# Attention and a PReLU MLP on one Trainium2 core: the first batch taken by halves of its queries, with a new order of the opening

## The chip, the cores and the metric

The kernel runs on one core of one Trainium2 chip. TensorE (PE) multiplies matrices and writes its results to PSUM; VectorE (DVE) and ScalarE (ACT) do element-wise work and read PSUM; GpSimd (POOL) does element-wise work in SBUF and issues part of the DMAs; SyncE (SP) issues the others. Every engine works off its own queue strictly in the order in which the kernel recorded its instructions. The metric is the device time of one execution in microseconds (us), as the median of several runs.

## What is computed

```python
q_n, k_n = rmsnorm(q, g_q), rmsnorm(k, g_k)          # (8, 12, 448, 64), over the last axis
attn = softmax(q_n @ k_n.T / 8);  o = attn @ v        # per batch and head
x = o.transpose(0, 2, 1, 3).reshape(3584, 768)
h = x @ w_in                                          # (768, 2048)
g = max(h, 0) + alpha * min(h, 0)
out = g @ w_out                                       # (2048, 768), float32
```

## The kernel before, in words

Each of the 8 batches has 12 heads, taken in three *groups* of four; group y is number y % 3 of batch y // 3, so groups 0, 1 and 2 are batch 0. The 448 queries or keys of a head are seven sets of 64. Everything is issued by a list of steps, PLAN (lines 24 to 190), that fixes the order on all engines at once. A step has a name, and its arguments say which group, set or column block it works on:

- `load_qk(y)` (line 286): q and k of a group by DMA from SP's queue, 448 KB each. A load waits until its buffer's last reader is done. `load_v`, `load_w_in(c)` (335), `load_w_out`: DMAs from POOL's queue that also turn the values into 16 bits. `load_w_in(c)` brings rows 0 to 511 of a quarter of w_in's columns in four DMAs and, for an even c, rows 512 to 767 of two quarters in four more.
- `square` (361; on POOL, in one case on ACT), `reduce` (378; DVE), `root` (408; ACT), `scale` (419; DVE or POOL), `turn` (543), `turn_one` (509): rms norm of a group's q and k and their transposes on PE, with copies out of PSUM on DVE. For group 0 the pieces are finer: `part_square`, `part_reduce`, `part_root`, `part_scale`, `part_turn`, `part_copy` (446 to 501).
- `opening` (1010): the first loads, the small DMAs of alpha, g_q and g_k into `rows`, idle matmuls (`spin`, 996: 2 wide float32 ones and 17 narrow 16-bit ones), and a transpose `ct` of `rows`; `gains` (1028) makes the product g_q * g_k, by which k is multiplied as it is copied to kT.
- `score(y,j)` (580): for key set j, the products with all 448 queries, for the group's four heads: four matmuls of 64x64 weights and 448 columns. `soft(y,j)` (599): exp on ACT, 128x896 values. Seven of each per group.
- `den` (645), `attend` (675): sums over the keys of exp, and of exp times v, with 64x32 weights; 56 matmuls each. Groups 0 and 1 are summed together ("0+1", with two `attend`), group 2 alone. `log` and `invert` (ACT) make 1/den as exp(-ln), `times` (693; DVE) multiplies and writes xT, the MLP's input, as 16 bits.
- `up(b,ft)` (746): one block of 128 of the 2048 hidden values for 448 tokens: six matmuls of 128x128 weights and 448 columns. `begin(ft)` (734) does the first four of the six ahead, from groups 0+1 alone. `slope` (757; ACT, three blocks on DVE) writes alpha*h, `larger` (770; DVE) the maximum of h and that. `down(tile,oh)` is the second product.

PSUM has eight banks in three pools: `pss`, two buffers of two banks, for scores; `psa`, one of two banks; `psf` (tag "mm"), two of one bank. The last argument of `score`, `den`, `attend` and `up` chooses the pool. A step that asks for a buffer waits until its last reader is done.

Of the kernel before, what the change touches and what calls it, by code (L numbers as in the profile page):

```python
# [20 lines left out]
GROUPS = ("den", "den_pre", "log", "log_pre", "invert", "attend", "times")  # L21
# [3 lines left out]
opening() part_square(q,0:1,0:7,act) part_square(q,1:2,0:7,act) part_reduce(q,0:1,0:7) spin(2,0)  # L25
part_reduce(q,1:2,0:7) part_root(q,0:7) part_square(k,0:2,0:3,act) part_scale(q,0:7,7,pool)
part_reduce(k,0:2,0:3) part_square(k,0:2,3:7,act) square(1,q) load_w_in(1) spin(1)
part_reduce(k,0:2,3:7) part_root(k,3:7) reduce(1,q) square(1,k) part_root(k,0:3) gains()
part_turn(q,r0-7) load_qk(3) spin(1,0) part_scale(k,0:3,3,vec) part_turn(k,r0-3)
part_scale(k,3:7,4,vec) part_copy(q,0:7,vec) part_turn(k,r3-7) load_v(0) reduce(1,k) follow(0,k)  # L30
square(2,q) part_copy(k,0:3,vec) part_copy(k,3:7,vec) root(1) square(2,k) score(0,0,0) soft(0,0)
reduce(2,q,0) score(0,4,1) load_w_in(0) score(0,3,0) spin(1) reduce(2,q,1) soft(0,3) score(0,1,0)
scale(1,k) scale(1,q) soft(0,4) score(0,2,0) soft(0,2) reduce(2,k) score(0,6,1) turn_one(1,q)
soft(0,1) turn_one(1,k) score(1,0,1) score(1,3,0) spin(1) score(1,2,0) soft(0,6) root(2) soft(1,0)
load_qk(4) soft(1,3) scale(2,k) scale(2,q) follow(2,q) square(3,q) square(3,k) load_w_in(2)
soft(1,2) score(0,5,1) score(1,1,0) soft(0,5) soft(1,1) score(1,5,0) turn(2) soft(1,5) score(1,6,1)
soft(1,6) reduce(3,q,None) score(1,4,0) score(2,0,0) soft(1,4) den(0+1,0) follow(1,k) soft(2,0)
log(0+1) load_qk(5) score(2,1,0) spin(1) reduce(3,k,0+1) attend(0+1,1,0) score(2,6,0) score(2,4,1)
attend(0+1,0,1) soft(2,1) root(3) score(2,3,1) invert(0+1) scale(3,q) scale(3,k) score(2,2,0)
load_w_in(3) soft(2,4) soft(2,6) times(0+1,1,0) times(0+1,1,1) square(4,q) times(0+1,0,0) turn(3)  # L40
score(2,5,0) square(4,k) load_qk(6) reduce(4,q,None) soft(2,3) soft(2,2) soft(2,5) den(2,0) log(2)
reduce(4,k,None) invert(2) attend(2,0,1) score(3,0,1) square(5,q) square(5,k) times(2,0,0)
score(3,1,0) begin(0) reduce(5,q) square(6,q) soft(3,0) begin(1) up(0,0,0) load_w_out(0) reduce(5,k)
up(0,1,0) begin(2) begin(3) root(4) up(0,2,0) up(0,3,1) up(0,4,0) scale(4,q) slope(0,0) soft(3,1)
larger(0,0) score(3,2,0) score(3,6,0) slope(0,1) load_qk(7) follow(2,k) larger(0,1) slope(0,4)
slope(0,2) slope(0,3) larger(0,4) up(0,5,0) larger(0,2) larger(0,3) root(5) soft(3,6) slope(0,5)
soft(3,2) larger(0,5) up(0,6,0) scale(4,k) turn(4) scale(5,q) up(0,8,0) score(4,0,0) slope(0,6)
score(4,1,1) square(6,k) larger(0,6) slope(0,8) score(3,5,0) up(0,9,0) load_w_out(1) scale(5,k)
soft(4,0) square(7,q) larger(0,8) up(0,11,0) load_qk(8) score(4,2,0) score(3,3,0) soft(3,5)
load_v(1) square(7,k) up(0,7,1) soft(4,1) slope(0,9) up(0,10,0) reduce(6,q) square(8,q) reduce(6,k)  # L50
load_w_out(2) soft(4,2) up(0,12,0) slope(0,11) larger(0,9) soft(3,3) score(3,4,0) slope(0,10)
score(4,3,0) larger(0,11) larger(0,10) slope(0,7) larger(0,7) up(0,13,0) soft(3,4) slope(0,12)
larger(0,12) turn(5) up(0,14,0) square(8,k) soft(4,3) score(4,6,0) slope(0,13) score(4,4,1) root(6)
slope(0,14) larger(0,13) up(0,15,0) scale(6,q) reduce(8,q) soft(4,4) score(5,4,0) larger(0,14)
scale(6,k) score(5,0,1) reduce(7,q) slope(0,15) larger(0,15) down(1,0,0) score(5,2,1) score(4,5,0)
soft(4,6) soft(5,0) soft(5,4) soft(5,2) score(5,1,0) soft(4,5) down(0,0,0) turn(6) load_w_out(3)
den(3+4,1) reduce(7,k) attend(3+4,0,0) score(5,5,0) score(5,6,0) soft(5,1) mix_weights(0,1) log(3+4)
invert(3+4) soft(5,5) soft(5,6) mix_weights(0,3) attend(3+4,1,0) score(6,0,1) score(5,3,0) soft(6,0)
score(6,4,0) down_end(0,0) down(2,0,0) soft(5,3) root(7) scale(7,q) load_qk(9) soft(6,4) scale(7,k)
den(5,0) attend(5,0,1) down_end(1,0) mix_weights(0,2) times(3+4,0,0) times(3+4,1,0) times(3+4,1,1)  # L60
load_qk(10) log(5) down(0,1,0) reduce(8,k) invert(5) down_end(2,0) times(5,0,1) times(5,0,0)
times(5,0,3) times(5,0,2) score(6,5,1) mix_weights(0,0) score(6,1,0) down_end(0,1) score(6,6,0)
soft(6,5) turn(7) up(1,1,1) square(9,q) down(1,1,0) root(8) reduce(9,q) soft(6,6) score(6,3,1)
score(7,0,0) slope(1,1) score(6,2,0) up(1,2,0) up(1,0,0) soft(6,1) soft(7,0) soft(6,3) square(9,k)
up(1,3,1) up(1,4,0) slope(1,2) slope(1,0) larger(1,1) down_end(1,1) reduce(9,k) root(9) larger(1,2)
load_qk(11) larger(1,0) slope(1,3) scale(8,q) soft(6,2) up(1,7,0) slope(1,4) larger(1,3) larger(1,4)
scale(8,k) score(7,4,0) slope(1,7) larger(1,7) up(1,5,1) scale(9,q) turn(8) score(7,5,0) soft(7,4)
score(7,1,0) up(1,6,0) square(10,q) slope(1,5) larger(1,5) up(1,10,0) soft(7,5) soft(7,1) up(1,8,1)
scale(9,k) up(1,9,0) reduce(10,q) score(7,2,0) slope(1,6) slope(1,10) larger(1,6) mix_weights(1,1)
score(7,6,0) slope(1,8) slope(1,9) soft(7,6) up(1,12,1) up(1,11,0) soft(7,2) square(10,k) up(1,13,0)  # L70
larger(1,8) larger(1,10) slope(1,12) score(7,3,0) larger(1,9) up(1,14,1) slope(1,11) slope(1,13)
mix_weights(1,3) reduce(10,k) up(1,15,0) load_v(2) soft(7,3) larger(1,12) load_qk(12) score(8,3,0)
score(8,0,0) den(6+7,0) slope(1,14) fold(10) root(10) slope(1,15) soft(8,0) down(2,1,0) larger(1,11)
larger(1,13) square(11,q) log(6+7) score(8,1,0) score(8,4,0) soft(8,3) flip(9,k) scale(10,q)
larger(1,14) larger(1,15) score(8,5,1) mix_weights(3,1) down_end(2,1) reduce(11,q) square(11,k)
# [16 lines left out]
soft(10,5) slope(2,13) larger(2,6) larger(2,8) larger(2,10) reduce(13,k) up(2,11,0) larger(2,5)
larger(2,12) load_qk(15) score(11,0,0) fold(13) den(9+10,1) slope(2,11) mix_weights(3,3) qa1(6,0)
up(2,15,0) qa2(6,1) root(13) mix_weights(3,0) flip(12,q) slope(2,9) larger(2,14) larger(2,13)
down(5,0,0) log(9+10) slope(2,15) larger(2,11) larger(2,9) invert(9+10) soft(11,0) square(14,k)
# [98 lines left out]
def kernel(  # L194
# [903 lines left out]
```

## Time and profile before

| | |
|---|---|
| median of 3 runs | 411.36 us (410.83 to 411.58) |
| the profiled execution | 410.69 us, of which the span is 408.6 us |
| busy: PE, DVE, ACT, POOL | 97%, 66%, 66%, 73% of the span |
| HBM read, written | 58.40 MB, 11.01 MB |

Busy time is the time in which an engine has an instruction at work; matmuls overlap each other, so a group's busy time can be less than count times mean. PEld is the weight load of PE, which runs beside its matmuls. In the timeline a line gives start, busy time, engine, source line, operation, tiles and shape, the number of merged instructions, and in brackets the engine's idle time before them with what ended it. Idle time of an engine that does not bound the kernel costs nothing.

### The profile page before, as it was taken

Reading aid. Unit: us, or ns where it says so; the run is one execution under the profiler, and the core shown is the slowest. Engines: PE = TensorE matmul, PEld = TensorE weight load, DVE = VectorE, ACT = ScalarE, POOL = GpSimd, SP = SyncE. Lnnn points to the kernel's source line nnn. Section 1 sums busy time; section 2 is a strip of 40 time slices with the busy share of each in tenths; the row PEclk is TensorE's granted clock in tenths of the full one; section 3 lists DMA queues with packets and bytes.
Section 4 is the critical chain, followed back from the end, with each engine's and each line's share of the span. In section 5 each row is a group of like instructions: output and inputs, shape, how many; then the busy total and the mean of one; then the engine's idle time right before and its main releaser. Section 6 shows DMA issues by size and latency. Waiting matters only on the chain.

```text
span 408.6 us, 11992 instructions
## 1 busy us (share of the span) xinstructions
PE 395.3 (97%) x5083; PEld 210.3 (51%) x5083; DVE 268.3 (66%) x480; ACT 270.4 (66%) x405; POOL 299.9 (73%) x200
## 2 busy tenths in 40 slices
PE   7688999999999999999999999999999999999996
PEld 3344445555455445554455455555555455655664
DVE  3957874676766685779678678886668545654422
ACT  5597686757885876767886987686876874245110
POOL 7977998497796998997796995589496809600780
PEclk9999999999999999999999999999999999999999
DMA  7999699796776794579952595794516000230143
GB/s 260 242 280 227 110 265 165 173 239 177 125 180 154 173 203 108 119 172 185 232 130 83 136 240 145 147 217 102 140 38 131 21 2 22 59 79 0 39 98 98
DMA packets 37222, 58.39 MB, mean 143 GB/s; under 512 B 4769, under 2 KB 28977, under 8 KB 37169
## 3 DMA queue, kind: packets, MB, share of 16 engines
q1 hardware_dynamic: 23232, 45.43, 43.2%
q0 software_dynamic: 13536, 11.81, 19.1%
q8 instruction: 39, 0.64, 0.7%
q10 hardware_dynamic: 400, 0.39, 0.3%
q14 instruction: 15, 0.11, 0.1%
HBM read 58.40 MB, written 11.01 MB: 170 GB/s over the span
## 4 chain that ended last, share of the span: by engine, by line
PE 88%; DVE 4%; DMA 3%; POOL 3%; issue 1%; POOLq 0%; DVEq 0%
PE hT L726 25%; PE hTa L726 9%; PE sc L588 8%; PE op L792 7%; PE qx L854 5%; PE av L613 5%; PE qz L854 4%; PE qc L854 4%; PE oq L854 4%; PE qxa L854 3%; PE avb L613 2%; PE dn L613 2%; PE oqm L854 2%; DMA w_in_sb<-in_moe_w_in_dram 2%; POOL nat L376 2%; DMA arena<-in_g_k_dram 2%
## 5 line engine op out<-in xcount | busy, mean ns | idle before, releaser
L602 ACT ACTIVATE expT<-sc 128x896 f16<-128x896 f32 x168 | 146.3, 916 | 40.9 <-PE sc L588 39.2
L726 PE MATMUL hT<-xT,w_in_sb 128*128 128x448 f16 x558 | 115.9, 353 | 1.6 <-DVE xT L709 1.4
L726 PEld LDWEIGHTS <-w_in_sb 128*128 128x128 f16 x768 | 73.0, 98 | 74.5 <-issue 9.9
L423 POOL TENSOR_TENSOR qs<-nat,rr 128x896 f16<-128x896 f32 x30 | 65.7, 2221 | 26.5 <-ACT rr L417 23.4
L766 ACT ACTIVATE gT<-hT,cols 128x448 f16<-128x448 f32 x92 | 58.4, 636 | 40.0 <-PE hT L726 38.9
L772 DVE TENSOR_TENSOR gT<-hT,gT 128x448 f16<-128x448 f32 x93 | 57.3, 619 | 38.2 <-ACT gT L766 37.5
L365 POOL TENSOR_TENSOR nat<-nat 128x896 f32<-128x896 f32 x30 | 50.7, 1697 | 8.1 <-DMA nat<-in_q_dram 7.7
L588 PE MATMUL sc<-qT,kT 64*32 64x448 f16 (+1 forms) x1092 | 49.4, 355 | 4.3 <-ACT expT L602 1.7
L854 PEld LDWEIGHTS <-gT 128*128 128x128 f16 x352 | 33.4, 98 | 25.5 <-issue 4.1
L726 PE MATMUL hTa<-xT,w_in_sb 128*128 128x448 f16 x198 | 42.9, 353 | 0.0
L842 POOL TENSOR_TENSOR gs<-gT 128x1024 f16<-128x1024 f16 x4 | 8.5, 2127 | 36.7 <-DVE gT L772 36.7
L709 DVE TENSOR_TENSOR xT<-av,rden 64x448 f16<-64x448 f32 (+1 forms) x37 | 27.2, 736 | 10.7 <-ACT rden L671 4.6
L386 DVE TENSOR_REDUCE sp<-nat 128x28 f32<-128x896 f32 x30 | 32.1, 1070 | 2.1 <-POOL nat L365 2.0
L588 PEld LDWEIGHTS <-kT 64*32 64x32 f16 (+1 forms) x1092 | 16.7, 93 | 32.4 <-issue 23.0
L792 PE MATMUL op<-w_out_sb,gT 128*128 128x384 f16 x176 | 30.3, 326 | 0.2 <-DVE xT L709 0.2
L766 ACT ACTIVATE gT<-hTa,cols 128x448 f16<-128x448 f32 x33 | 21.0, 636 | 10.5 <-PE hTa L726 10.0
L772 DVE TENSOR_TENSOR gT<-hTa,gT 128x448 f16<-128x448 f32 x33 | 20.4, 618 | 10.6 <-ACT gT L766 10.2
L613 PEld LDWEIGHTS <-vt 64*32 64x32 f16 x1344 | 19.7, 92 | 12.2 <-issue 1.9
L792 PEld LDWEIGHTS <-gT 128*128 128x128 f16 x192 | 18.3, 98 | 14.5 <-issue 3.0
L613 PE MATMUL av<-expT,vt 64*32 64x448 f16 x896 | 24.3, 350 | 0.0
L850 POOL TENSOR_TENSOR gT<-gT 128x1024 f16<-128x1024 f16 x11 | 23.5, 2133 | 0.0
L854 PEld LDWEIGHTS <-arena 128*128 128x128 f16 x136 | 12.6, 98 | 10.5 <-issue 2.3
(151 smaller groups left out, 572.5 us busy)
## 6 DMA issues: line engine op xcount, KB each, us to landing
nat<-in_q_dram SPq DMA_DIRECT2D x60, 216.0 KB, 4.1
nat<-in_k_dram SPq DMA_DIRECT2D x60, 216.0 KB, 5.0
out_dram<-osb SPq DMA_DIRECT2D x107, 96.0 KB, 3.1
vt<-in_v_dram POOLq DMA_DIRECT2D x8, 672.0 KB, 7.8
w_in_sb<-in_moe_w_in_dram POOLq DMA_DIRECT2D x24, 128.0 KB, 7.3
w_out_sb<-in_moe_w_out_dram POOLq DMA_DIRECT2D x4, 768.0 KB, 8.6
nat<-in_k_dram SPq DMA_DIRECT2D x6, 448.0 KB, 7.8
nat<-in_q_dram SPq DMA_DIRECT2D x5, 448.0 KB, 6.7
```

Source lines behind the costliest of these rows:

```text
L365: nc.gpsimd.tensor_mul(out=sqs[y, nm], in0=t[:, :, :HD], in1=t[:, :, :HD])
L386: nc.vector.tensor_reduce(out=parts[y][:, ts("qk".index(nm), 4 * J), :1], in_=sqs[y, nm], axis=AXIS_X, op=ALU.add,)
L423: nc.gpsimd.tensor_mul(out=t.rearrange("p j d n -> p n j d"), in0=nat[y, nm][:, :, :HD].rearrange("p (n j) d -> p n j d", j=J), in1=r.unsq ...
L588: nc.tensor.matmul(out=sc[ds(64 * g + m * c, m), par, :S].rearrange("p (j c) -> p j c", j=J), lhsT=kT[ds(64 * par, 64), j, g, ts(c, m)], r ...
L602: nc.scalar.activation(out=expT[y][:, j], in_=scs[y, j][:, :, :S], func=AF.Exp, scale=QK_SCALE, bias=EXP_BIAS,)
L613: nc.tensor.matmul(out=accs[g][ds(32 * n, 32), :S], lhsT=weights(g, y, par, c, j), rhs=expT[y][ds(64 * g, 64), j, par, :], start=(j == 0), ...
L709: nc.vector.tensor_mul(out=o, in0=p, in1=q)
L726: nc.tensor.matmul(out=hT[:, :S], lhsT=w_in_sb[:, block_of(g, i), ts(ft, 128)], rhs=xT[b][:, g, i, :], start=(i == 0 and g == 0), stop=(i ...
L766: nc.scalar.activation(out=g, in_=hT[:, :S], func=AF.Copy, scale=alpha_sb[:, ft : ft + 1])
L772: nc.vector.tensor_max(out=g, in0=hT[:, :S], in1=g)
L792: nc.tensor.matmul(out=op[:, :OH], lhsT=gT[:, ft, ts(tile % J, 128)], rhs=w_out_sb[:, ft, ts(oh, OH)], start=(ft == 0), stop=(ft == NF - 1),)
L854: nc.tensor.matmul(out=bank[:, c], lhsT=g[:, ft], rhs=v[:, ft, c], start=(first and ft == 0), stop=(ft == HF - 1), skip_group_check=True,)
```

## The change

Batch 0 is computed in two halves of its queries, and everything up to group 8 stands in a new order: the first 458 steps of the new list replace the first 434 of the old one; the 891 steps from `score(9,5,0)` on are the same in both.

- **Half-query steps.** The half s holds queries 32s to 32s+31 of each set of 64, 224 in all. `score2(y,n,s)` takes key sets 2n and 2n+1 against half s in eight matmuls of 224 columns, into the two banks that one `score` uses, and `soft2` is one exp of 128x896 for them. Key set 6 is still scored whole by `score(y,6)`. So a group has six `score2` and one `score` in place of seven `score`.
- `den2`, `log2`, `invert2`, `attend2`, `times2` do for one half what their namesakes do for all queries: 56 matmuls of 224 columns for each `den2` and `attend2` of group 2, and 112 for `attend2(0+1,s)`, which puts both head halves side by side in one pair of banks.
- `begin2(f,s)` and `up2(f,s)` replace `up(0,ft)` for the first eight hidden blocks: blocks 2f and 2f+1 for one half, twelve matmuls of 224 columns into one bank, with one start flag for the pair. `slope2` does 224 columns of one block, on ACT or, in six of sixteen cases, on DVE; `larger2` does both blocks at once. Blocks 8 to 15 stay `up(0,ft)`. Fourteen of the later `slope` steps name DVE.
- **Opening.** No wide idle matmuls: 4 and 17 narrow ones at the start, then 2, 2, 4, 1, 2 and 3 narrow ones between the scores (before: 2, then 1 wide, 1 narrow, and three times 1 wide). g_q and g_k come first on POOL's queue, in two DMAs in place of four, then alpha. The transpose of `rows` is a step of its own (`factors`), after q of group 0 is transposed; `gains` comes after k's scaling on DVE. `part_root(k)` is one call ahead of `square(1,q)`. `square(1,k)`, `square(2,q)` and `part_copy(q)` go to ACT, `square(1,k)` and `square(2,q)` from POOL, the copy from DVE.
- **DMAs.** `load_w_in(c, lo, hi)` takes some of the eight DMAs: the rows 512 to 767 of quarters 0 and 1 come first, then v, then `square(3,k)` on POOL, then rows 0 to 511 of quarters 0 and 1.

The core of the diff, and the steps of the list up to the first MLP units:

```diff
-    def load_w_in(c):
+    def load_w_in(c, lo, hi):
+        for m in range(lo, hi):
...
+    def score2(y, n, s, spare=False):
+        qT, kT = qkT[y, "q"], qkT[y, "k"]
...
+        for e in range(2):
+            for par in range(2):
+                for g in range(2):
+                    nc.tensor.matmul(
+                        out=wide(sc[ds(64 * g, 64), par, ts(e, SH)]),
+                        lhsT=kT[ds(64 * par, 64), 2 * n + e, g, :],
+                        rhs=qT[ds(64 * par, 64), :, g, ts(s, 32)],
+                        start=True, stop=True,
+                    )
...
+    def up2_part(hT, f, s, lo, hi):
+        for e in range(2):
+            for i in range(lo, hi):
+                for g in range(2):
+                    nc.tensor.matmul(
+                        out=hT[:, ts(e, SH)],
+                        lhsT=w_in_sb[:, block_of(g, i), ts(2 * f + e, 128)],
+                        rhs=part(xT[0][:, g, i, :], s),
+                        start=(e == 0 and i == 0 and g == 0),
+                        stop=(i == G - 1 and g == 1), skip_group_check=True,
+                    )
...
+    def factors():
+        ct = pss.tile([128, 2, 512], FP32, name="ct", tag="sc")[:, 0]
```

```text
opening() spin(4,0) part_square(q,0:1,0:7,act) part_square(q,1:2,0:7,act) part_reduce(q,1:2,0:7)
part_reduce(q,0:1,0:7) part_root(q,0:7) part_square(k,0:2,3:7,act) part_square(k,0:2,0:3,act)
part_scale(q,0:7,7,pool) spin(17,0) part_reduce(k,0:2,3:7) part_turn(q,r0-7) part_reduce(k,0:2,0:3)
factors() part_root(k,0:7) square(1,q,act) load_w_in(0,4,8) part_scale(k,0:3,3,vec) square(1,k,act)
load_qk(3) part_turn(k,r0-3) part_copy(q,0:7,act) square(2,k) part_scale(k,3:7,4,vec) load_v(0)
gains() part_turn(k,r3-7) part_copy(k,0:3,vec) score2(0,0,0,0) part_copy(k,3:7,vec)
square(2,q,act,2) square(3,k,pool,2) soft2(0,0,0) reduce(1,k) score2(0,2,1,0) score2(0,1,0,1)
reduce(1,q) soft2(0,1,0) reduce(2,q,0) spin(2,0) root(1) score(0,6,0) load_w_in(0,0,4) spin(2,0)
score2(0,2,0,1) reduce(2,q,1) scale(1,q) soft2(0,2,1) load_w_in(1,0,4) load_qk(4) scale(1,k)
score2(0,1,1,0) soft2(0,2,0) spin(4,0) reduce(2,k) turn_one(1,q) score2(0,0,1,0) spin(1,0)
square(3,q) soft2(0,1,1) soft(0,6) root(2) turn_one(1,k) soft2(0,0,1) score2(1,0,0,0) soft2(1,0,0)
score(1,6,1) score2(1,1,0,0) spin(2,0) score2(1,2,0,0) soft2(1,1,0) square(4,k,pool,2) scale(2,q)
scale(2,k) spin(3,0) turn(2) load_qk(5) square(4,q) score2(1,0,1,0) soft2(1,2,0) load_w_in(2,4,8)
soft(1,6) score(2,6,1) score2(2,1,0,0) score2(2,2,0,0) soft2(1,0,1) soft(2,6) attend2(0+1,0,0)
reduce(3,k,0+1) load_w_in(2,0,4) soft2(2,1,0) score2(2,0,0,0) soft2(2,2,0) soft2(2,0,0)
den2(0+1,0,1) log2(0+1,0) den2(2,0,2) invert2(0+1,0) reduce(3,q,None) log2(2,0) square(5,q)
reduce(4,k,None) invert2(2,0) score2(1,1,1,1) times2(0+1,0,0) root(3) attend2(2,0,2) score2(1,2,1,0)
times2(0+1,0,1) soft2(1,1,1) times2(2,0,0) load_w_in(3,0,4) begin2(1,0) up2(1,0,2) score2(2,0,1,0)
score2(2,1,1,1) begin2(0,0,2) soft2(1,2,1) square(5,k,pool,2) slope2(1,0,1) scale(3,k) slope2(1,0,0)
up2(0,0,0) scale(3,q) larger2(1,0) turn(3) den2(0+1,1,1) load_w_out(0) score2(2,2,1,0) soft2(2,1,1)
begin2(2,0) up2(2,0) soft2(2,0,1) begin2(3,0,0) slope2(0,0,1) load_qk(6) slope2(0,0,0,vec)
log2(0+1,1) invert2(0+1,1) larger2(0,0) attend2(0+1,1,2) soft2(2,2,1) slope2(2,0,1) den2(2,1,2)
reduce(4,q,None) slope2(2,0,0) reduce(5,q) times2(0+1,1,1) root(4) attend2(2,1,1) scale(4,q)
scale(4,k) square(6,q,pool,2) log2(2,1) score(3,1,0) times2(0+1,1,0) invert2(2,1) larger2(2,0)
score(3,0,0) up2(3,0,2) soft(3,0) times2(2,1,0) slope2(3,0,1) slope2(3,0,0) begin2(0,1) up2(0,1)
```

More of the change, by code (lines that the diff above doesn't have):

```diff
@@ L34 @@
[L34 to L45, printed above, removed]
@@ L52 @@
[L52 to L63, printed above, removed]
@@ L92 @@
[L92 to L95, printed above, removed]
-flip(12,k) reduce(14,q) weigh(12) qa1v(6) larger(2,15) mix_weights(2,1) scale(13,q) score(11,3,1)
-scale(13,k) score(11,4,0) attend(9+10,0,1) mix_two(6,pool) soft(11,4) qa2v(6) mix_rest(6)
```

321 lines of the change are left out of this document (232 added, 89 removed).

## The prediction

> **What bounds the kernel now.** I read the page first, then the busy time by stretches, then the timeline of the first 50 us.
>
> ```profile
> PE 395.3 (97%) x5083; PEld 210.3 (51%) x5083; DVE 268.3 (66%) x480; ACT 270.4 (66%) x405; POOL 299.9 (73%) x200
> PE   7688999999999999999999999999999999999996
> PEclk9999999999999999999999999999999999999999
> ```
>
> PE is busy for 97% of the span, and the slices show where it is not: in the first four of 40 and in the last, where the final transfers end.
>
> ```profile
> 10.00:20.00 10.00, 6.75 (x64) 3.31 (x64) 9.91 (x17) 5.74 (x10) 9.44 (x13) 1.00 1.17 245
> 40.00:50.00 10.00, 8.77 (x62) 4.65 (x61) 8.60 (x14) 6.10 (x12) 9.98 (x8) 1.00 0.56 82
> 50.00:100.00 50.00, 49.63 (x629) 26.05 (x627) 32.91 (x53) 36.53 (x55) 38.98 (x27) 1.00 0.97 207
> ```
>
> (Columns: PE, PEld, DVE, ACT and POOL busy, clock, DMA share, GB/s.) From 50 us on PE has no idle time worth naming. So whatever PE gains or loses up to there is carried to the end, since the work behind it is the same. The opening is limited otherwise:
>
> ```profile
> 14.68 4.97 ACT L602 ACTIVATE expT<-sc 128x896 f16<-128x896 f32 x6 [0.30 <-PE sc L588]
> 20.24 7.50 ACT L602 ACTIVATE expT<-sc 128x896 f16<-128x896 f32 x9 [0.23 <-PE sc L588]
> 38.37 1.69 PE L726 MATMUL hT<-xT,w_in_sb 128*128 128x448 f16 x8
> 39.16 1.09 DVE L395 TENSOR_REDUCE ss<-nat 128x14 f32<-128x896 f32 x1 [0.55 <-POOL nat L376]
> 40.16 1.08 DVE L709 TENSOR_TENSOR xT<-av,rden 128x896 f16<-128x896 f32 x1
> 41.30 0.92 PE L726 MATMUL hT<-xT,w_in_sb 128*128 128x448 f16 x4 [1.23 <-DVE xT L709]
> 42.05 2.43 PE L726 MATMUL hTb<-xT,w_in_sb 128*128 128x448 f16 x12
> ```
>
> ACT takes an exp every 0.83 us (4.97/6, 7.50/9) and batch 0 has 21 of them. The first MLP matmul comes at 38.37, and the MLP flows only from 41.30, after a reduce that waited for POOL stood on DVE ahead of the last xT. By 42.05 + 2.43 = 44.48 PE has done 24 MLP matmuls, four units of six. That is my mark: **four MLP units, all of batch 0's attention, group 3 turned and two of its scores, at 44.48.**
>
> **The change, step by step.**
>
> *Narrow matmuls.* Nearest rows: group 5's den, already 56 matmuls of 224 columns; an attend of 448; transposes, each with a load of 128 weight columns.
>
> ```profile
> 79.08 0.86 PE L637 MATMUL dn<-expT,ones 64*32 64x224 f16 x56
> 79.77 1.51 PE L613 MATMUL av<-expT,vt 64*32 64x448 f16 x56
> 23.24 0.95 PE L560 MATMUL tps<-ident,qs 128*128 128x128 f16 x14
> 142.65 2.27 PE hT L726 x12
> L726 PEld LDWEIGHTS <-w_in_sb 128*128 128x128 f16 x768 | 73.0, 98 | 74.5 <-issue 9.9
> ```
>
> The narrow 56 hand over after 79.77 - 79.08 = 0.69 us, half of a wide 56: no penalty. A wide MLP matmul takes 2.27/12 = 0.19 us, so a narrow one should take 0.095, if its weight load keeps up. A load takes 0.098 by itself, but load plus transpose go at 0.95/14 = 0.068, so most of a load hides. So eight narrow units of 12 x 0.095 = 1.14 cost what eight wide ones cost: nothing added. Bounds: nothing, and 0.01 exposed in each of the 96. [...]
>
> *Start of the exps.* Rows of before:
>
> ```profile
> 6.58 1.04 ACT L450 ACTIVATE nat<-nat 128x384 f32<-128x384 f32 x2 [1.01 <-DMA nat<-in_k_dram]
> 7.13 1.21 DVE L457 TENSOR_REDUCE ss<-nat 128x6 f32<-128x384 f32 x2 [2.06 <-ACT nat L450]
> 8.32 0.95 ACT L370 ACTIVATE nat<-nat 128x896 f32<-128x896 f32 x1 [0.70 <-DMA nat<-in_q_dram]
> 10.20 0.20 PE L1025 MATMUL ct<-ident,arena 18*128 18x18 f32 x1 [1.07 <-DMA arena<-in_g_k_dram]
> 11.19 1.15 DVE L474 TENSOR_TENSOR qs<-nat,rr 128x384 f16<-128x384 f32 x2
> 13.90 0.23 ACT L416 ACTIVATE rr<-ss 128x28 f32<-128x28 f32 x1 [3.94 <-DVE ss L395]
> 14.24 0.96 PE L588 MATMUL sc<-qT,kT 64*64 64x448 f16 x12 [1.37 <-DVE kT L495]
> ```
>
> In before, k's root stood behind group 1's square on ACT, and gain behind the last of four small DMAs, which landed at 10.2. In after, k's reduces end as before, near 8.4; its root follows at once (two ACT operations of 0.23, so a root is 0.5) and ends at 8.9, its scaling (1.15) at 10.05. q's swapped reduces delay q by half a square, 0.5, which nothing waits for: k comes later. Two of the four gain DMAs are gone and the rest go ahead of alpha: `ct` is ready between 9 and 10.2, PE has turned k by 10.6 or 10.7, and kT's first part is there by 11.1 at the latest. But ACT has first two squares (0.95 each), then the q copy that the first score needs (not shown on ACT; between nothing beside the squares and twice an exp's 0.83; I take 0.9, as it reads as many values from PSUM), and two half squares (1.1 for both, a little over a whole one) before the first exp: 8.9 + 1.9 + 0.9 + 1.1 = 12.8; I say 12.7, as back to back ACT operations overlap a little. **First exp 12.7 instead of 14.7.** A narrow score counts like a wide one. The idle matmuls stand where PE waits for ACT; 14 of them at 0.19 (448 columns, as the wide MLP matmul) are 2.7 us in 15 us, hidden by ACT's 0.83 per exp; without that cover they would cost all 2.7.
>
> *To the first MLP unit.* Before the first half is done ACT needs 16 exps, two roots and one wait. Seven exps are group 0's, both halves; nine are group 1's and 2's. The wait: `turn_one(1,k)` gets the PSUM buffer of `turn_one(1,q)`, since a `spin` stands between, so k's transposes wait for DVE's q copy.
>
> ```profile
> 15.55 2.41 DVE L436 TENSOR_TENSOR arena<-nat,rr 128x896 f16<-128x896 f32 x2
> 18.88 0.61 DVE L519 COPY qT<-tps 128x896 f16<-128x896 f16 x1
> 19.41 0.79 DVE L523 TENSOR_SCALAR kT<-tps,gain 128x256 f16<-128x256 f16 x2
> 80.02 0.54 ACT L666 ACTIVATE rden<-dn 128x448 f32<-128x448 f32 x1 [1.10 <-PE dn L637]
> 80.60 0.58 ACT L671 ACTIVATE rden<-rden 128x448 f32<-128x448 f32 x1
> ```
>
> DVE: root 1 done at 14.8, two scalings (2.4) to 17.2, a reduce (1.1) to 18.3, q copy 18.9, transposes (0.5), first k copy 19.8; group 1's first exp at 20.35, 0.7 after ACT was free. Then nine exps, 7.5, to 27.9; log 0.54 and invert 0.58 to 29.0; two `times2` of 448 values (half of the 1.08 above, each with some fixed part: 0.6) to 30.2. **First MLP unit at 30.2 instead of 38.4.**
>
> *From there PE is full.* It has: four units, 4 x 1.14 = 4.56; five scores, 0.45 each with their fill (12 matmuls of before take 0.96), 2.25; `turn(3)` 0.95; two narrow dens 1.4; attends 1.4 + 0.7. Sum 11.26: the mark at 30.2 + 11.3 = 41.5. ACT in that time has five exps, two pairs of log and invert, two roots and nine narrow slopes (bounded by half and whole of the wide slope's 0.64 in the next fence; I take 0.4): about 11; it keeps up. 44.48 - 41.5 = **3.0 us gained**.
>
> *What I take off.* POOL and SP:
>
> ```profile
> 12.41 0.37 SPq L306 DMA_DIRECT2D nat<-in_k_dram  x1
> 15.96 2.22 POOL L339 DMA_DIRECT2D w_in_sb<-in_moe_w_in_dram  x4
> 35.80 3.33 POOL L376 TENSOR_TENSOR nat<-nat 128x896 f32<-128x896 f32 x2
> nat<-in_k_dram SPq DMA_DIRECT2D x6, 448.0 KB, 7.8
> w_in_sb<-in_moe_w_in_dram POOLq DMA_DIRECT2D x24, 128.0 KB, 7.3
> DMA to landing us min/median/max: 2.6/6.9/11.3
> 41.87 0.63 ACT L766 ACTIVATE gT<-hT,cols 128x448 f16<-128x448 f32 x1 [1.11 <-PE hT L726]
> ```
>
> In after, group 3's k is asked for at 10.1 rather than 12.41 and lands some 7 later. `square(3,k)` waits for it on POOL (some 3 us idle), and behind it stand eight w_in issues (0.55 each), `square(3,q)` and both of group 4. That gives: squares of k to 19, first quarter issued by 21.2 and landed by 29, second by 31; `square(4,k)` done at 27 to 29, as group 4's k takes 7 or near 10 to land. DVE's reduce of it stands ahead of the first `times2`, so xT is free of it at 28 to 30: 0 to 1 us lost, I take 0.5. The splits of units and the shorter stretches of one kind on PE add fill: between 0 and 1, I take 0.3. Behind the mark, 20 slopes on DVE (three before) let PE wait for a bank here and there: between 0 and 2 us up to group 8, I take 0.3, as `slope` and `larger` then follow without a hand-over. Sum: 3.0 - 1.1 = **1.9 us**. The profiled execution gives 410.69 - 1.9 = 408.8; the median is 0.67 higher, so **409.5 us**.
>
> **The rivals.**
>
> 1. *More:* POOL is on time and nothing is lost behind the mark: 3.0, and near 1 more if the squares on ACT overlap as exps do and `ct` comes early. About 407.4. For it: PE's 1.23 idle at 41.30 came from an order that is gone. Chance 0.13.
> 2. *Hidden or given back:* DVE is at 8.6 of 10 in 40:50 already, and takes slopes on top; PE then waits for banks 2 us more between 45 and 110: 411.2. Against it: 6.6 of 10 over the span. 0.15.
> 3. *Weight loads bound the narrow units:* a load of 0.098 beside a stream of 0.095 leaves 0.01 exposed in each of 96 matmuls, 1.0 us: 410.5. Against it: 0.068 for load and transpose. 0.05. [...]
> 4. *Slower, by POOL's queue:* group 3's k takes the longest landing shown, 11.3: 10.1 + 11.3 = 21.4, squares (1.8) to 23.2, four issues to 25.4, the last of the first quarter lands up to 9.6 later (the median at 18 to 21 us in the fence below), 35.0. PE's queue stands at the first unit for 4.8 us: 2.4 - 4.8, or 413.8. It decides from a landing after 32.6 (30.2 + 2.4); a middle case gives 412.8. The DMA share of 1.17 in 10:20 speaks for it; that quarter 0's last rows are asked for before v, in a quiet queue, speaks against. 0.15.
> 5. *Slower, by the clock:*
>
> ```profile
> w_in_sb<-in_moe_w_in_dram POOLq DMA_DIRECT2D x5, 128.0 KB, 9.6
> 5.37 0.15 PEld L1000 LDWEIGHTS <-ident 128*128 128x128 f16 x1 [0.22 <-issue]
> 6.86 1.82 PEld L1000 LDWEIGHTS <-ident 128*128 128x128 f16 x10 [0.22 <-issue]
> ```
>
> The idle matmuls come 0.37 apart until 6.86 and 0.18 after: PE runs at half rate first, though the clock row shows 9. If after's thinner opening fell back to that, the attends, dens and turns on the path would take 3.3 more (1.4 + 0.7 + 1.2): 412.8. Before's idle of 1.37 ahead of its first score did not do that. 0.07. [...]
>
> **How the numbers follow.** Forecast 0.45, between 408.5 and 410.5. A measurement tells about 0.2%, 0.8 us, from no change. Faster: 0.45 + 0.13 = 0.58; same: rivals 2 and 3, 0.20; slower: 4 and 5, 0.22. The range, 407.0 to 413.0, leaves out the far ends of rivals 1, 4 and 5.
>
> **What would show it.** Right: first exp near 12.7, first MLP matmul near 30.2 released by xT, PE busy 9.5 of 10 from 30 on, `dn` of 224 columns in 0.69, units in 1.14. Wrong: the first unit waits for w_in or for a reduce behind POOL (4), L1157 or L615 matmuls at double spacing after 12 us (5), PE idle of over 1 us between 45 and 110 (2), units over 1.2 (3).

## The result, and the profile after

The median is **422.89 us** (421.60 to 424.86, 4 runs) against 411.36: 1.029 times the kernel before (95% interval 1.024 to 1.033). The forecast was 409.5, faster; the kernel is some 11.5 us slower, outside the range, and by a mechanism that none of the rivals named. The profiled execution took 421.6 us, with a span of 419.8.

The page of the kernel after, sums and slices:

```profile
PE 398.8 (95%) x5486; PEld 219.4 (52%) x5486; DVE 278.9 (66%) x498; ACT 265.6 (63%) x402; POOL 296.1 (71%) x197
...
PE   7758699999999999999999999999999999999995
...
PEclk9999799999999999999999999999999999999999
```

Beside the lines of before, PE has 403 more matmuls, with as many more weight loads. Its busy time grew by 3.5 us (398.8 - 395.3), its idle time by 7.7 (21.0 of 419.8 against 13.3 of 408.6). The slices place most of the new idle time in 20 to 60 us, and the view by stretches (columns as in the prediction's fence) shows that the granted clock was down there too, from 30 us on. The first row is of the kernel before, the others of the kernel after:

```profile
20.00:30.00 10.00, 8.51 (x157) 4.38 (x160) 5.57 (x9) 9.70 (x15) 7.69 (x12) 1.00 1.12 282
...
20.00:30.00 10.00, 5.26 (x227) 3.79 (x235) 5.08 (x7) 6.10 (x8) 8.31 (x11) 1.00 1.12 263
30.00:40.00 10.00, 8.37 (x225) 6.09 (x215) 6.84 (x8) 7.04 (x13) 9.98 (x15) 0.83 0.97 154
40.00:50.00 10.00, 7.50 (x300) 5.81 (x285) 5.79 (x10) 4.34 (x10) 7.14 (x7) 0.86 1.16 273
50.00:60.00 10.00, 8.92 (x82) 7.27 (x82) 5.41 (x10) 6.20 (x12) 0.70 (x1) 0.80 0.62 96
60.00:100.00 40.00, 39.71 (x557) 20.92 (x555) 29.82 (x49) 26.78 (x41) 29.82 (x23) 1.00 0.90 182
```

In 20:30, where before had PE busy for 8.51 us, it is now busy for 5.26. What PE waited for (total, times, longest) begins with a releaser that this view of the kernel before doesn't have for PE at all:

```profile
PE dn L647 <- issue: 4.1, 1, 4.1
PE av L647 <- issue: 2.6, 2, 2.2
```

"issue" is time in which nothing that the profile shows held PE back. A fourth such stop, of 1.30 us, is in the MLP (`hT`). The four places in PE's timeline:

```profile
24.90 0.76 PE L647 MATMUL dn<-expT,ones 64*32 64x224 f16 x45
29.79 1.62 PE L647 MATMUL dn<-expT,ones 64*32 64x224 f16 x67 [4.13 <-issue]
31.35 0.59 PE L615 MATMUL sc<-qT,kT 64*64 64x224 f16 x8
31.86 1.50 PE L647 MATMUL av<-expT,vt 64*32 64x224 f16 x53
33.80 0.27 PE L647 MATMUL av<-expT,vt 64*32 64x224 f16 x3 [0.43 <-issue]
...
34.32 1.32 PE L705 MATMUL hT<-xT,w_in_sb 128*128 128x224 f16 x12
35.57 0.58 PE L615 MATMUL sc<-qT,kT 64*64 64x224 f16 x16
...
46.42 0.29 PE L647 MATMUL av<-expT,vt 64*32 64x224 f16 x8 [2.17 <-issue]
46.52 0.96 PE L647 MATMUL dn<-expT,ones 64*32 64x224 f16 x56
47.19 1.58 PE L647 MATMUL av<-expT,vt 64*32 64x224 f16 x56
48.71 0.96 PE L749 MATMUL sc<-qT,kT 64*64 64x448 f16 x8
50.97 3.14 PE L705 MATMUL hT<-xT,w_in_sb 128*128 128x224 f16 x16 [1.30 <-issue]
```

PE stops in the middle of a sum, 45 matmuls into `den2(0+1,0)`, with its bank open, and goes on without anything that the profile shows releasing it. Count from the first stop to the second: 67 + 8 + 53 = **128 matmuls**. From the third to the fourth: 8 + 56 + 56 + 8 = 128. (Between the second and the third the trace has 253, about two such stretches, and no stop where they meet.) With one weight load each that is 256 instructions. The page lists a DMA queue that carries instructions (packets, MB, share); its line in the kernel before and in the kernel after:

```profile
q8 instruction: 39, 0.64, 0.7%
```

```profile
q8 instruction: 43, 0.70, 0.7%
```

5083 matmuls with their loads are 10,166 instructions, 39.7 times 256; 5486 are 10,972, 42.9 times 256. So a packet of this queue is one block of 256 of PE's instructions, some 16 KB (0.70 MB / 43). **Theory A: PE's instructions arrive in such blocks, the next one is fetched only when PE enters the one before, and where 128 matmuls take less time than the fetch, PE stands at the block's edge until it is there.** Theory B: narrow matmuls as such, or waits that the profile doesn't name, cost the time. Theory C, for what is left: the opening, with less work for PE, lets the clock fall.

### The profile page after: what moved, and what is told of

The parts are those of the page before. It is cut to its first block, busy times and chain, and to the rows that moved or that the text cites. A ratio compares the mean times of both kernels' runs of the same rounds, so it can differ in the third digit from the quotient of the medians.

```text
span 419.8 us, 12811 instructions
## 1 busy us (share of the span) xinstructions
PE 398.8 (95%) x5486; PEld 219.4 (52%) x5486; DVE 278.9 (66%) x498; ACT 265.6 (63%) x402; POOL 296.1 (71%) x197
## 4 chain that ended last, share of the span: by engine, by line
PE 86%; DVE 5%; ACT 4%; issue 3%; DMA 1%; SPq 0%; DVEq 0%; ACTq 0%
PE hT L883 22%; PE hTa L883 9%; PE sc L749 8%; PE op L949 7%; PE qx L1011 5%; PE av L770 4%; PE qz L1011 4%; PE qc L1011 4%; PE oq L1011 3%; PE qxa L1011 3%; PE avb L770 2%; PE dn L770 2%; PE oqm L1011 2%; PE hT L705 2%; PE qza L1011 1%
## 5 line engine op out<-in xcount | busy, mean ns | idle before, releaser
L759 ACT ACTIVATE expT<-sc 128x896 f16<-128x896 f32 x150 | 130.7, 915 | 44.5 <-PE sc L749 42.8
L883 PE MATMUL hT<-xT,w_in_sb 128*128 128x448 f16 x510 | 106.1, 353 | 0.3 <-DVE xT L866 0.2
L883 PEld LDWEIGHTS <-w_in_sb 128*128 128x128 f16 x720 | 68.6, 98 | 69.9 <-issue 9.9
L929 DVE TENSOR_TENSOR gT<-hT,gT 128x448 f16<-128x448 f32 x85 | 52.6, 620 | 33.8 <-ACT gT L923 32.9
L923 ACT ACTIVATE gT<-hT,cols 128x448 f16<-128x448 f32 x74 | 46.9, 635 | 33.9 <-PE hT L883 33.1
L883 PE MATMUL hTa<-xT,w_in_sb 128*128 128x448 f16 x210 | 45.4, 352 | 0.6 <-DVE gT L929 0.5
L749 PE MATMUL sc<-qT,kT 64*32 64x448 f16 (+1 forms) x1020 | 43.6, 356 | 1.8 <-DVE kT L578 0.8
L866 DVE TENSOR_TENSOR xT<-av,rden 64x448 f16<-64x448 f32 (+1 forms) x35 | 25.1, 716 | 9.6 <-ACT rden L828 4.5
L923 ACT ACTIVATE gT<-hTa,cols 128x448 f16<-128x448 f32 x32 | 20.3, 635 | 13.4 <-PE hTa L883 13.3
L770 PEld LDWEIGHTS <-vt 64*32 64x32 f16 x1176 | 17.0, 92 | 10.0 <-issue 1.1
L770 PE MATMUL av<-expT,vt 64*32 64x448 f16 x784 | 21.2, 349 | 0.0
L1011 PEld LDWEIGHTS <-arena 128*128 128x128 f16 x136 | 12.7, 98 | 10.5 <-issue 2.6
```

The costliest lines, as they stand in the source:

```text
L749: nc.tensor.matmul(out=order(y, sc[ds(64 * g + m * c, m), par, :S]), lhsT=kT[ds(64 * par, 64), j, g, ts(c, m)], rhs=ordered(y, qT[ds(64 * ...
L759: nc.scalar.activation(out=exps(y)[:, j], in_=scs[y, j][:, :, :S], func=AF.Exp, scale=QK_SCALE, bias=EXP_BIAS,)
L770: nc.tensor.matmul(out=accs[g][ds(32 * n, 32), :S], lhsT=weights(g, y, par, c, j), rhs=expT[y][ds(64 * g, 64), j, par, :], start=(j == 0), ...
L866: nc.vector.tensor_mul(out=o, in0=p, in1=q)
L883: nc.tensor.matmul(out=hT[:, :S], lhsT=w_in_sb[:, block_of(g, i), ts(ft, 128)], rhs=xT[b][:, g, i, :], start=(i == 0 and g == 0), stop=(i ...
L923: nc.scalar.activation(out=g, in_=hT[:, :S], func=AF.Copy, scale=alpha_sb[:, ft : ft + 1])
```

## The experiments

**1. The edges moved.** The 17 idle matmuls of the start become 34 of half the columns:

```diff
-        for _ in range(count):
+        cut = 2 if count == 17 else 1
+        for _ in range(count * cut):
             nc.tensor.matmul(
-                out=ps[:, :S], lhsT=idle32[:, :128] if wide else ident,
-                rhs=idle32 if wide else idle, start=True, stop=True,
+                out=ps[:, : S // cut], lhsT=idle32[:, :128] if wide else ident,
+                rhs=idle32 if wide else idle[:, : S // cut], start=True, stop=True,
```

> The 17 idle matmuls of 448 columns at the start become 34 of 224: the same PE time, 34 more PE instructions ahead of everything else. Theory A (PE's instructions come in blocks of 256, the next block is late when transfers are dense, and PE stops at the block's edge): the stop inside the first half's den moves from after its 45th matmul to after its 28th, 17 earlier, and is again 3 to 5 us long; the stop in the second half's attend moves from after matmul 104 to after matmul 87. Time 420 to 425 us. Theory B (something in the den itself is waited for: a bank, a flag, an exp): the stop stays after the 45th matmul. Theory C (the clock falls first, for want of wide idle matmuls, and the rest follows): no stop of whole microseconds before the clock falls.

424.19 us in one run (before: 411.97 median on that chip). PE's timeline:

```profile
25.18 0.56 PE L647 MATMUL dn<-expT,ones 64*32 64x224 f16 x28
30.16 2.24 PE L647 MATMUL dn<-expT,ones 64*32 64x224 f16 x84 [4.42 <-issue]
...
44.27 1.25 PE L647 MATMUL av<-expT,vt 64*32 64x224 f16 x87
47.69 0.57 PE L647 MATMUL av<-expT,vt 64*32 64x224 f16 x25 [2.17 <-issue]
```

17 matmuls added 20 us earlier, the stop 17 matmuls earlier in the same sum: 28 in place of 45. The stop in the second half's `attend2` moved in the same way, from after 104 matmuls to after 87, as expected. A wait on data or on a bank would have stayed where it was. This is theory A's sign, and it rules theory B out for these stops.

**2. Fewer transfers.** Eight w_in loads are left out (rows 0 to 511 of quarters 0 and 1 are zeros, so the output is not the reference's):

```diff
+    nc.vector.memset(w_in_sb[:, :4, : 2 * FB], 0.0)
-reduce(1,q) soft2(0,1,0) reduce(2,q,0) spin(2,0) root(1) score(0,6,0) load_w_in(0,0,4) spin(2,0)
-score2(0,2,0,1) reduce(2,q,1) scale(1,q) soft2(0,2,1) load_w_in(1,0,4) load_qk(4) scale(1,k)
+reduce(1,q) soft2(0,1,0) reduce(2,q,0) spin(2,0) root(1) score(0,6,0) spin(2,0)
+score2(0,2,0,1) reduce(2,q,1) scale(1,q) soft2(0,2,1) load_qk(4) scale(1,k)
```

> Leaves out the eight loads of w_in's rows 0 to 511 of the first two quarters (the MLP then multiplies zeros there); PE's instructions are the same. Theory A: the block that was late by 4.1 us has fewer transfers ahead of it, so the stop after the 45th den matmul shrinks to under 2 us, and the time falls by 2 to 6 us against the changed kernel. Theory B: the stop is as long as before, 4 us.

421.53 us in one run. The DMA share in 20 to 30 us fell from 1.12 to 0.58, and the first stop, at the same matmul (67 of the 112 are left), from 4.13 to 0.96 us:

```profile
28.41 1.04 PE L648 MATMUL dn<-expT,ones 64*32 64x224 f16 x67 [0.96 <-issue]
```

Later, with the traffic back at a share of 1.07, the stops at `attend2` were 5.1 us in sum (2.6 in the kernel after): one stop was eased and the next ones took its place. The total was 1.4 us under the kernel after's median, on another chip and in one run, short of the 2 to 6 that were expected. The second stop also kept its matmul, the third and fourth came two matmuls later. So a stop's length goes with the transfers beside it; its place hardly does.

**3. Fewer instructions, same columns.** In `den2` and `attend2` seven narrow matmuls become three of 448 columns, which read a half twice, and one of 224. The sums are not the attention's, so the output isn't the reference's; 240 matmuls fewer.

```diff
-        for j in range(J):
+        for j in (0, 2, 4, 6):
...
+                    r = 1 if j == 6 else 2
...
-                        rhs=expT[y][ds(64 * g, 64), j, par, ts(s, SH)],
+                        rhs=one.unsqueeze(1).broadcast_to((64, r, SH)),
```

> Each seven narrow matmuls of a half's den and attend (224 columns) become three of 448, which read the same half twice, and one of 224: the sums are not the attention's, the streamed columns and PE's time are the same, and the ten sums have 320 matmuls instead of 560, 480 PE instructions fewer. Theory A: between the block edges PE has more time, the stops shrink from 8 us in all to under 2, the clock stays near 1, and the kernel takes 408 to 412 us, as the prediction's walk had it. Theory B: the stops stay where they are. Theory C: the clock still falls and the time stays over 418.

417.25 us (416.71 to 417.81; 1.013 times before, interval 1.010 to 1.017): 5.6 us better than the kernel after, but 408 to 412 was expected. PE's timeline shows what was left: stops of 1.78 and 1.09 us before 45 us, and one where nothing had been changed, in group 8's and 9's steps:

```profile
263.09 0.85 PE L797 MATMUL dnb<-expT,ones 64*32 64x224 f16 x56
263.76 1.51 PE L773 MATMUL av<-expT,vt 64*32 64x448 f16 x56
265.09 0.55 PE L752 MATMUL sc<-qT,kT 64*32 64x448 f16 x11
267.19 0.37 PE L752 MATMUL sc<-qT,kT 64*32 64x448 f16 x5 [1.56 <-issue]
```

123 matmuls in 2.5 us, and then a stop. By theory A the number of instructions ahead decides where the edges fall in all that follows. In the kernel after, and in that before, PE has no such stop there; here it has one. PE's stops put down to issue are 4.8 us in sum (2.9 + 1.9), of 6.9 by which the span is longer than before's (415.5 - 408.6). The clock, which was expected to stay near 1, was 0.66 in 10 to 20 us, ahead of any stop, and 1.00 from 20 to 60.

**4. The new opening alone.** The new list up to group 0's first scores, then the old one, with whole scores and wide units:

```diff
-opening() part_square(q,0:1,0:7,act) part_square(q,1:2,0:7,act) part_reduce(q,0:1,0:7) spin(2,0)
...
-reduce(2,q,0) score(0,4,1) load_w_in(0) score(0,3,0) spin(1) reduce(2,q,1) soft(0,3) score(0,1,0)
+opening() spin(4,0) part_square(q,0:1,0:7,act) part_square(q,1:2,0:7,act) part_reduce(q,1:2,0:7)
...
+square(2,q,act,2) soft(0,0) reduce(1,k) score(0,4,1) score(0,3,0)
+reduce(1,q) soft(0,3) reduce(2,q,0) root(1) spin(1) load_w_in(0,0,8) score(0,1,0) reduce(2,q,1)
 scale(1,k) scale(1,q) soft(0,4) score(0,2,0) soft(0,2) reduce(2,k) score(0,6,1) turn_one(1,q)
```

> One part of the change alone: the new opening up to the first score (gain first, k's root before group 1's squares, squares and q's copy on ACT), with whole scores and the old order behind it. Theory A: exps start near 12 instead of 14.7, no stop of PE's instructions of over 1 us, as a den is 56 matmuls of 448 columns again; 409 to 411.5 us. Theory C (the thinner idle matmuls of the opening let the clock fall): granted clock under 1 and over 414 us.

411.9 us (10 runs; ratio 1.000, interval 0.997 to 1.002). No stop put down to issue, but no gain either. ACT's timeline has the first exp at 12.40, 2.3 us ahead of before, and group 1's first at 19.44, only 0.8 ahead; and the clock is down:

```profile
12.40 1.71 ACT L749 ACTIVATE expT<-sc 128x896 f16<-128x896 f32 x2
...
19.44 1.73 ACT L749 ACTIVATE expT<-sc 128x896 f16<-128x896 f32 x2 [1.30 <-PE sc L739]
22.20 2.54 ACT L749 ACTIVATE expT<-sc 128x896 f16<-128x896 f32 x3 [1.04 <-PE sc L739]
```

```profile
15.00:18.00 3.00, 1.91 (x17) 1.46 (x17) 2.98 (x4) 2.97 (x6) 2.65 (x6) 0.50 1.17 227
```

**5. The supply measured by itself.** A kernel that computes nothing of the reference: matmuls of 64x32 weights and 224 columns with nothing to wait for, first without transfers ("quiet"), then beside loads from both queues ("busy"), then 448 columns ("wide").

```diff
+    t = stream("quiet", 140, 224, x)
+    traffic(t[:, 0, :8], 12)
+    t = warm(34)
+    t2 = stream("busy", 70, 224, z)
+    t3 = stream("wide", 35, 448, z)
```

> Not the reference's computation: it writes one constant tile, and only TensorE's own stream is read. First 1120 matmuls of 224 columns with nothing to wait for and no transfers (2240 instructions, weight loads counted), then 34 of 448 columns, then 560 of 224 columns while SyncE and GpSimd load 448 KB and 128 KB pieces as hard as the opening does, then 280 of 448 columns. Theory A (TensorE's instructions come in blocks of 256, that is 128 matmuls with their loads, and the next block is fetched only when the one before is entered): gaps that the profile puts down to issue, 128 matmuls apart; with transfers one block takes 3 to 6 us against the 1.8 us that its matmuls take, so a gap of 1.5 to 4 us at each edge; without transfers the fetch takes under 2 us and the gaps are below 0.7 us. With 448 columns (128 matmuls at some 24 ns more each) the gaps are shorter by the longer block. Theory B (narrow matmuls as such are slow, or the stops came from waits that the profile does not name): no gaps at a period of 128 matmuls, in either stream.

```profile
11.67 1.73 PE L53 MATMUL quiet<-x,ones 64*32 64x224 f16 x128 [1.72 <-issue]
15.12 1.73 PE L53 MATMUL quiet<-x,ones 64*32 64x224 f16 x128 [1.73 <-issue]
...
50.47 3.19 PE L53 MATMUL busy<-z,ones 64*32 64x224 f16 x128 [4.21 <-issue]
56.66 3.19 PE L53 MATMUL busy<-z,ones 64*32 64x224 f16 x128 [3.01 <-issue]
...
69.05 8.10 PE L53 MATMUL wide<-z,ones 64*32 64x448 f16 x259 [2.90 <-issue]
```

Every 128 matmuls PE stops, in the quiet part with nothing else at work. A block takes 15.12 - 11.67 = **3.5 us without transfers** (up to 3.7 in the rows left out) and 56.66 - 50.47 = **6.2 us beside them**, while its matmuls need 1.73 at full clock. Only the size of the quiet stops was misjudged, 1.7 to 2.0 us in place of under 0.7. The last row holds 259 matmuls of 448 columns without a stop, when few transfers were left; 128 of them took some 4 us (8.10 / 259 x 128, 31 ns each against 1.73 / 128 = 13.5 ns of a narrow one in quiet, at a clock of 0.76 to 0.92 in 70 to 80 us), longer than a quiet block's 3.5.

The trace also has the instruction queue's packets, one for each block. In quiet one starts 0.9 to 1.4 us after an edge (between 12.60 and 12.80 behind the edge at 11.67), beside transfers 3.9 to 4.1 (between 54.40 and 54.60 behind 50.47), and PE goes on 2.1 to 2.8 us after the packet's start in either part: what the transfers lengthened here is the time until the packet. The block entered at 36.67 lasted some 8 us, because it began with the last 25 quiet matmuls and the 34 longer ones of 448 columns between the streams. It got a single packet, between 37.80 and 38.00; the next came between 48.00 and 48.20, and PE stood one block later, up to 50.47. So not even in 8 us was a second block fetched ahead, which is the other half of theory A.

After the stop of 4.21 us the clock is down to 0.50, in each 5 us from 50 to 65, while the stops of 3.01 us go on (through the quiet part's stops of 1.72 to 2.00 us it was 1.00):

```profile
50.00:55.00 5.00, 3.19 (x128) 2.89 (x128) 0.00 (x0) 1.81 (x4) 0.50 1.15 283
```

Of a block's time the stop is 1.7 us of 3.5 in quiet and 3.0 of 6.2 beside transfers.

**6. The kernel before, with more instructions.** Its order, opening and exps; only the sums and attention of groups 0 to 2 have each matmul cut into two:

```diff
+        cut = 2 if ys[0] < 3 else 1
+        for s in range(cut):
...
-                        out=accs[g][ds(32 * n, 32), :S],
+                            out=accs[g][ds(32 * n, 32), ts(s, S // cut)],
```

> The kernel before with its order, opening, exps and waits; only the sums and attention of the first batch (groups 0, 1 and 2) have each matmul cut into two of 224 columns: 280 more matmuls, 560 more instructions of TensorE, the same columns in sum. Theory A (TensorE waits for its instruction blocks of 256): stops put down to issue at the new edges inside this part, the likeliest ahead of the score after the second attention (about 34 us) and 106 of 112 matmuls into group 2's sums (about 36 us), 1 to 3 us each, and 413 to 416 us in all. Theory B (the prediction's own step: twice as many matmuls of half the columns cost the same): 411 to 412 us, no such stops.

**425.55 us** (422.74 to 427.76; 1.030, interval 1.025 to 1.035), slower than the kernel after, and further up than expected. PE's timeline:

```profile
31.07 1.55 PE L615 MATMUL avb<-expT,vt 64*32 64x224 f16 x99
36.38 0.38 PE L615 MATMUL avb<-expT,vt 64*32 64x224 f16 x13 [3.76 <-issue]
36.69 0.57 PE L588 MATMUL sc<-qT,kT 64*64 64x448 f16 x8
37.19 2.45 PE L615 MATMUL av<-expT,vt 64*32 64x224 f16 x107
42.85 0.38 PE L615 MATMUL av<-expT,vt 64*32 64x224 f16 x5 [3.21 <-issue]
...
53.81 0.57 PE L588 MATMUL sc<-qT,kT 64*64 64x448 f16 x7 [3.59 <-issue]
```

13 + 8 + 107 = 128 again; from one stop's end to the next 6.5 us. This is one part of the change alone, in the old order, and it costs as much as the whole change: the stops (10.9 us in sum) and the clock after them (0.61 in 40 to 50 us; PE busy 402.7 us in sum, 7.4 more than before). Not all of it need be the split's. The profiled execution, at 427.56, is one of the two longer of four, and its clock was also down ahead of the first stop, 0.83 in 20 to 30 us and 0.51 in 21 to 24, where ACT waited 1.22 us for scores and nothing had been changed yet.

**7. The new opening, kept warm.** Experiment 4 with 13 more idle matmuls at 8 to 12 us:

```diff
-part_scale(q,0:7,7,pool) spin(17,0) part_reduce(k,0:2,3:7) part_turn(q,r0-7) part_reduce(k,0:2,0:3)
+part_scale(q,0:7,7,pool) spin(21,0) part_reduce(k,0:2,3:7) part_turn(q,r0-7) spin(3,0) part_reduce(k,0:2,0:3)
...
-load_qk(3) part_turn(k,r0-3) part_copy(q,0:7,act) square(2,k) part_scale(k,3:7,4,vec) load_v(0)
-gains() part_turn(k,r3-7) part_copy(k,0:3,vec) score(0,0,0) part_copy(k,3:7,vec)
+load_qk(3) part_turn(k,r0-3) spin(2,0) part_copy(q,0:7,act) square(2,k) part_scale(k,3:7,4,vec) load_v(0)
+gains() part_turn(k,r3-7) spin(4,0) part_copy(k,0:3,vec) score(0,0,0) part_copy(k,3:7,vec)
```

> The kernel of the experiment with the new opening alone, with 13 more idle matmuls of 448 columns at 8 to 12 us (4 before the first turning of q, 3 and 2 around k's, 4 ahead of the first scores), to keep the clock up. Theory C (the new opening saves about 2 us at the first exp, and the clock that fell to 0.5 between 12 and 24 us gives it back): clock 1.00 through 30 us and 409.3 to 410.8 us. Rival (the first part is set by ScalarE's and VectorE's own rows and by the loads, not by the clock, or the idle matmuls delay what they stand ahead of): 411 to 412.5 us, no difference to the kernel before that can be told.

413.49 us (12 runs; ratio 1.004, interval 1.001 to 1.006): slightly slower, and above both expectations. The clock was 1.00 until 18 us; then it fell, to 0.92 in 18 to 21 us and further behind that:

```profile
15.00:18.00 3.00, 0.77 (x8) 0.22 (x7) 3.00 (x6) 2.95 (x7) 3.00 (x6) 1.00 0.99 157
...
21.00:24.00 3.00, 2.92 (x14) 0.83 (x15) 1.30 (x2) 1.84 (x3) 1.89 (x3) 0.52 1.05 232
```

The added matmuls stand ahead of k's transposes and the first scores, and the first exp came at 13.30, 0.9 us later than in experiment 4. Group 1's first exp came at 20.34, where before has 20.24. From the first exp to that one it is 7.04 us here and 7.04 in experiment 4 (19.44 - 12.40), at a clock of 1.00 up to 18 us here and of 0.50 to 0.63 there; before needs 5.56 (20.24 - 14.68). So in this stretch, where the opening loses 1.5 of its 2.3 us, theory C, the clock as what ate the gain, falls. DVE (third pair) is busy for all of 15 to 18 us here, and for 2.98 of 3.00 in experiment 4: it works off group 1's and 2's reduces and scalings. That DVE's row of work sets group 1's first scores fits both runs, but was not tried by itself.

Right behind it theory C is not out. In both runs the clock is down at 21 us (0.67 and 0.52 in 21 to 24), the two wide idle matmuls ahead of group 1's next scores take 1.86 us (1.02 before), and group 1's third exp waits for its scores, 1.04 us in experiment 4 and 1.16 here; the kernel before has no wait there. That is about what experiment 4 had left of its lead, 0.8 us, and no run of this opening with whole scores kept the clock up there.

**8. An edge put where it should hurt the kernel before.** Its 17 idle matmuls become 105 of 56 columns, 88 more:

```diff
-        for _ in range(count):
+        w = S if count != 17 else 56
+        for _ in range(count if count != 17 else 105):
```

> The kernel before, with one edit: the 17 idle matmuls of 448 columns at 4 to 8 us are 105 of 56 columns, 88 more matmuls (176 more instructions) at a place where TensorE waits for q in any case. Nothing later is changed. Theory A: the edges between TensorE's blocks of 256 instructions move by 88 matmuls, so that one falls at the first matmul of the first sums (26.2 us in the kernel before) and the next 128 matmuls on, about 3 matmuls into the second attention (31.1 us). That block then lasts 4.9 us, where the separate measurement gives 6.2 us for the fetch of a block beside transfers: a stop put down to issue of 0.5 to 2 us there, the likeliest a second one of 0.3 to 1.5 us near the end of group 2's sums (128 matmuls on), and 412.5 to 415.5 us in all. Theory B (a shift of the instructions costs nothing, the kernel before is not sensitive to it): 411.2 to 412.2 us and no stop put down to issue.

411.46 us (10 runs; ratio 0.997, interval 0.994 to 1.001): the same. PE's timeline:

```profile
27.87 1.56 PE L613 MATMUL dn<-expT,ones 64*32 64x448 f16 x56 [0.43 <-ACT expT L602]
...
36.92 1.62 PE L613 MATMUL dn<-expT,ones 64*32 64x448 f16 x49
39.42 0.38 PE L613 MATMUL dn<-expT,ones 64*32 64x448 f16 x7 [0.88 <-issue]
...
41.56 2.44 PE L726 MATMUL hT<-xT,w_in_sb 128*128 128x448 f16 x12
```

The second of the two stops is there, near the end of group 2's sums, 0.88 us. The first is not. If the edges lie where they were expected, the block before it lasts 4.9 us from 27.87, and the next one was fetched in that time (its packet starts between 30.20 and 30.40): a fetch beside transfers, at a DMA share of 1.11 to 1.15, took less than 4.9 here. And the stop cost nothing in the end: the wait of 1.23 us for xT, which the kernel before has in its first MLP units, is gone from the row of 12. The expected total, 412.5 to 415.5, was a miss: the stop of 0.88 us stood ahead of a wait that was longer than it.

No version here beats the kernel before by more than a measurement can tell.

## Why the prediction was wrong, point by point

*Start of the exps: right in kind, better in size.* First exp at 11.88 in the kernel after, forecast 12.7. It is worth little by itself (experiment 4).

*To the first MLP unit: right up to the stop.* ACT's timeline in the kernel after:

```profile
11.88 1.71 ACT L629 ACTIVATE expT<-sc 128x896 f16<-128x896 f32 x2
...
18.60 2.54 ACT L629 ACTIVATE expT<-sc 128x896 f16<-128x896 f32 x3 [0.18 <-PE sc L615]
...
23.62 2.53 ACT L629 ACTIVATE expT<-sc 128x896 f16<-128x896 f32 x3
30.21 0.54 ACT L665 ACTIVATE rden<-dn 128x448 f32<-128x448 f32 x1 [4.06 <-PE dn L647]
```

Group 1's first exp was forecast for 20.35 and came at 18.60; the first half's last exp ended at 23.62 + 2.53 = 26.15, forecast 27.9. The walk was then 1.75 us ahead of the forecast. But the log of the first half waited 4.06 us for sums that stood at a block's edge, and the first unit came at 34.32 in place of 30.2.

***Narrow matmuls*, "nothing added": the step that failed.** The row it rests on was read rightly: a narrow `dn` hands over after 47.19 - 46.52 = 0.67 us, forecast 0.69. A unit takes 35.57 - 34.32 = 1.25 with its hand-over to scores, and a later one 58.27 - 57.11 = 1.16 up to the transposes behind it; forecast 1.14. What the step left out is that a narrow matmul is as many instructions as a wide one. With whole scores and sums 128 matmuls of the dense part took 4.9 us in experiment 8, about what a block took in the kernel after with its stop, 4.0 and 4.6; in halves they can need little more than the 1.73 us of experiment 5 where `attend2`, `den2` and scores stand back to back (`attend2` and a score, 120 matmuls, from 23.12 to 24.90 in the kernel after: 1.78 us). The group 5 `dn` from which the price came is a single sum between wide matmuls, and shows nothing of this. Experiment 6 shows the term alone: 280 more matmuls with the same columns cost 13 us, of which the early fall of the clock can be some 1 us.

*"From there PE is full": wrong for the same reason.* After the first unit PE stops for 2.17 and 1.30 us more. The last four matmuls of the mark's fourth unit come only at 50.97, behind group 3's two scores, where before had the whole mark at 44.48 and the forecast at 41.5.

*What I take off.* POOL's queue and the banks were not what decided. From 60 to 200 us PE is idle for 1.3 us in sum, 0.9 more than before, against a forecast loss of 0.3 behind the mark; that is far from the 2 us of the second rival. DVE's two scalings at 34.73 took 3.81 us together (2.41 in before's row) and held `turn(3)` for 1.19 us; that is a size that was missed, beside 8.0 us of stops.

*The rivals.* Clock: it did fall, to 0.80 to 0.86 in 30 to 60 us, but behind stops, not by the thinner opening; in 10 to 30 us it was 1.00 in the profiled execution of the kernel after. Behind the first stop, 4.13 us long, the clock is 0.52 in 30 to 33 us. The idle time of 1.37 us in the kernel before, named there against this rival, doesn't settle it: in experiment 4, where no wait of PE is over 1.5 us, the clock was 0.50 in 15 to 18 us. Weight loads: units at 1.16 to 1.25 are 0.2 to 0.9 us more in eight, at most near that rival's 1.0. No run shows its 0.01 us exposed in each matmul; the two rows it names differ by 0.003 (0.098 - 0.095), 0.3 us in 96. Neither gives 11 us.

The sum, by spans: 8.0 us of stops and 3.5 us more busy time of PE (slower clock and units, not separated), less 0.3 of other idle time that went, are the 11.2 us (419.8 - 408.6).

## What to carry to other kernels

Before work is cut into more and shorter matmuls, count TensorE's instructions: for each stretch of 128 matmuls with their loads, compare its time with a block's fetch, here 3.5 us in quiet and 4 to 6.5 us beside dense transfers (all measured in the first 70 us of their kernels). Where the stretch was shorter, TensorE stopped at its end (1.73 us of matmuls and a stop of 1.72 in the quiet part of experiment 5), and the clock could be down behind it (0.52 behind a stop of 4.13 us); the sign in a profile is idle time put down to issue, 128 matmuls apart, here also in the middle of a sum. In experiment 1, 17 more matmuls moved two later stops by 17, and experiment 3 has a stop of 1.56 us at 267 us where nothing had been changed, so a stop far behind an edit may be its doing.

## What the runs showed of the hardware that was not expected

- One block of 256 instructions of TensorE takes 3.5 to 3.7 us without transfers, 6.2 beside them in the separate measurement, 6.5 in experiment 6; in experiment 8 one came within 4.9. In the kernel after it was 33.80 - 29.79 = 4.0 and 50.97 - 46.42 = 4.6.
- After a stop of 4.13 us the clock fell, to 0.52 in 30 to 33 us, and after one of 2.17 us too: 0.79 in 46 to 48 and 0.80 in 50 to 60 us, where the fourth stop followed soon. Which of the two brought the second fall was not separated.
- The clock also fell with no stop ahead of it: experiment 4, where no wait of PE is over 1.5 us, had 0.50 at 15 to 18 us; experiments 6 and 7 had 0.51 and 0.52 at 21 to 24 us, and experiment 6 has the opening of the kernel before, whose own profile had 1.00 there. What decides this is open.
